# A retention and mixture-of-experts kernel: operand places within 256 bytes, and one load issued earlier

## The chip, the cores and the metric

The kernel runs on one core of a Trainium2 chip. The metric is the device time of one execution in microseconds. TensorE multiplies, VectorE (DVE) and ScalarE (ACT) do elementwise work, GpSimd (POOL) gathers and scatters rows, and SyncE (SP) issues nearly all DMAs from one queue, in order.

## The reference

Three layers in a row on 4608 tokens of width 512, all in float32:

```python
scores = scale * np.matmul(q, k.transpose(0, 1, 3, 2))       # 8 batches, 8 heads, 576 x 64
ret = scores * Dmat[None]                                    # decay gamma**(i-j), causal
x = np.matmul(ret, v)                                        # -> (4608, 512)

logits = x @ w_gate + modality_bias[modality_id]             # 8 experts, top 1
for e in range(8):
    h = np.maximum(x[mask] @ w1[e], 0.0)                     # 512 -> 1024
    out[mask] = gate_w[mask, None] * (h @ w2[e])             # 1024 -> 512

h = np.maximum(x @ w_in, 0.0)                                # 512 -> 2048
return (h * h @ w_out).astype(np.float32)                    # 2048 -> 512
```

## The kernel before

Every float32 operand of the big products is split in a high and a low part, and a product is three matmuls: high by high, high by low, low by high. In a matmul one operand is stationary (128 columns are loaded) and the other streams past it.

Stage 1 (to about 200 us) computes the retention and the routing. Stage 2 computes the experts. A unit is a slot of up to 512 tokens of one expert with one of 8 groups of 128 hidden columns; units are numbered i = 0 to 79, and the slots are 512 tokens wide, at the end 448 (i = 56 to 63), 384 (64 to 71) and 256 (72 to 79). Pass i of the loop issues `first` of unit i + 1 (lines 839 to 841; ACT makes hh at 855, VectorE hl at 856), in some passes `trans` of the next slot's tokens (ACT xh, VectorE xl, 794 and 795), then `second` of unit i, then a split of expert weights (ACT at 156, VectorE at 157) and a share of the generator `convs`. That one prepares the last stage's weights in 16 conversions (VectorE at 745 to 768, then `conv3`, which splits them in cwh and cwl and stores them). ACT, VectorE and SP each work through their queue in this order of issue. A third generator, `combos`, makes the first token sums of the last stage: its first step empties `convs`, takes two tiles and issues the load of eyr (line 802); the later steps compute on eyr. Its steps are taken at i = 65 (one) and from 66 on (two each). By the costs that `convs` gives for its pieces, four block sums and the first half of `conv3` come at i = 62 and the other half at 63.

Stage 3 (from about 616 us) is the last layer pair, in Strassen-like form: 9 blocks of 512 tokens, seven products each, hidden columns in three passes. In the first layer (`one`) the weights w are stationary and the tokens' sums x stream, 256 columns a matmul; in the second (`two`) h is stationary and the weights stream, 256 columns. Both issue their three matmuls in the helper `six` (lines 1199 to 1201). The order of all work in stage 3 is written out by a planner from fixed costs and due times; addresses play no part in it.

Where tiles stand: the pools `cv` (6 tiles of 8192 bytes in each partition), `wp` (10 of 8192), `rp` (one of 8192) and `ip` (three of 32) follow each other, and then, in stage 3, the pool with h0, h1 and h2. All tiles of `cv` and `wp`, and so x and both layers' weights, have the same place within 256 bytes; the h tiles, 14336 bytes each, stand 96 bytes beyond it. The stage-2 tiles of tokens and of h have the place of the weights.

Of the kernel before, what the change touches and what calls it, by code (L numbers as in the profile page):

```python
# [10 lines left out]
F32R = mybir.dt.float32r  # L11
# [14 lines left out]
P = 128  # L26
# [66 lines left out]
def kernel(ctx, tc, qT, kT, kN, vN, modT, w_gate, mbias, w1, w2, w_in, w_out,  # L93
# [155 lines left out]
    def route_c(g):  # L249
        t0 = G * g  # L250
        ob, ok = RS.pop(g)
        for j in range(G):
            pe.matmul(tps, ob[:, j, :], ok[:, j, :], start=(t0 + j == 0), stop=True, skip_group_check=True)

    def tab_out():
        dve.tensor_scalar(out=tab, in0=tps, scalar1=IDOFF, scalar2=None, op0=ALU.add)
# [155 lines left out]
    def run(gen, n):  # L412
        for _ in range(n):
            if next(gen, 0) == 0:
                return False
        return True

    def chain(*gens):
        for g_ in gens:
            for _ in g_:  # L420
                yield 1
# [45 lines left out]
    def gather(s):  # L467
        nt = blocks(s)
        rmax = (NTILE - G) * P if s == "E" else NT
        src = eslot[0:1, 1:2] if s == "E" else slots[0:1, 1, s:s + 1]  # L470
        reg = pool.value_load(src, min_val=0, max_val=KEYS - nt)
        ix = new(ip, [P, 4], I32, "ix", "ix")
        pool.tensor_copy(ix[:, :nt], tab[:, bass.ds(reg, nt)])
        xg = new(wp, [P, 4, DM], F32, "w", "xg")
        for j in range(nt):
            pool.indirect_dma_start(out=xg[:, j, :], out_offset=None, in_=xd[:rmax, :],
                                    in_offset=bass.IndirectOffsetOnAxis(ap=ix[:, j:j + 1], axis=0))
        XG[s] = (xg, ix)
# [236 lines left out]
    def phase12():  # L715
        ring[0] = psG
        with ExitStack() as c1:
# [79 lines left out]
            def combos():  # L797
                for _ in cs:
                    pass
                yr = cv.tile([P, KD, TS], F32, tag="w", name="eyr")  # L800
                tx = cv.tile([P, 2, 256], F32, tag="w", name="etx")
                sp.dma_start(yr, yd[:, 0:TS].rearrange("(c p) t -> p c t", p=P))
                yield 1
                xs = [cv.tile([P, 2, 2, 2, 256], F32R, tag="w", name=f"x{a}") for a in range(4)]
                b11, b12 = yr[:, 0:2, 0:256], yr[:, 0:2, 256:512]
                b21, b22 = yr[:, 2:4, 0:256], yr[:, 2:4, 256:512]

                def sub(o, a, b):
                    dve.tensor_tensor(out=o, in0=a, in1=b, op=ALU.subtract)

                def put(m, src):
                    t_ = held["x", m] = xs[m // 2][:, m % 2]
                    split(t_[:, 0], t_[:, 1], src, dve)
                    sp.dma_start(xc[0, m], t_.bitcast(F32).rearrange("p a k t -> p (a k t)"))

                sub(tx, b12, b11)
                put(0, b11)
                yield 1
                put(1, b21)
                yield 1  # L820
                sub(b12, b22, b12)
                put(2, b22)
                yield 1
                sub(b11, b22, tx)
                put(3, tx)
                yield 1
                put(5, b12)
                yield 1
                sub(b21, b21, b11)
                put(4, b11)  # L830
                yield 1
                put(6, b21)
                yield 1
# [9 lines left out]
            def first(u):  # L843
                s, f = u
                xh, xl = X[s]
                wd = width(s)
                w = W[s, f // 2][0]
                fo = slice((f % 2) * P, (f % 2) * P + P)
                ps = new(psG, [P, TS], F32, "g", "psh")[:, :wd]
                for k in range(KD):  # L850
                    three(ps, (w[:, 0, k, fo], w[:, 1, k, fo]), (xh[:, k, :wd], xl[:, k, :wd]),
                          k == 0, k == KD - 1)
                hh = new(hp, [P, TS], F32R, "hh", "hh")[:, :wd]
                hl = new(hp, [P, TS], F32R, "hl", "hl")[:, :wd]
                act.activation(hh, ps, AF.Relu)
                dve.scalar_tensor_tensor(out=hl, in0=ps, scalar=0.0, in1=hh.bitcast(F32), op0=ALU.max,  # L856
                                         op1=ALU.subtract)
                HS[u] = (hh, hl)
# [37 lines left out]
            ex = combos()  # L896
# [9 lines left out]
            def ws(upto, most=99, ldto=0):  # L906
                while most and st["sp"] < min(upto, nw):
                    wl(st["sp"] + 1)
                    wsplit(wkeys[st["sp"] // 2], st["sp"] % 2, dve)
                    st["sp"] += 1  # L910
                    most -= 1
                    wl(ldto)
# [90 lines left out]
            for i, u in enumerate(us):  # L1003
                s, f = u
                k = seq.index(s)
                nx = seq[k + 1] if k + 1 < len(seq) else None
                if nx is not None and f == (4 if s == "E" else 0):
                    gather(nx)
                if i + 1 < len(us):
                    first(us[i + 1])  # L1010
                if nx is not None:
                    if s == "E" and f == 6:
                        trans(nx, 0)
                        trans(nx, 1)
                    elif s != "E" and 3 <= f <= 6:
                        trans(nx, f - 3)
                if u == (NF, 7):
                    wload2(1, 0, wp)
                if i == 71:
                    tc.mark_branch_hint_location("extra0", 0, HINTED)  # L1020
                second(u)
                if s == "E" and f == 6:
                    trans(nx, 2)
                    trans(nx, 3)
                if i == 2:
                    route_c(last)
                if i == 0:
                    for _ in route_a(last):
                        pass
                    next(cs)  # L1030
                elif i == 1:
                    tb = table()
                    next(tb)
                    for _ in route_b(last, dve):
                        next(tb)
                elif i == 2:
                    ws(6, 2, 7)
                    tab_out()
                    turn = tab_turn()
                    next(turn)  # L1040
                    for _ in range(10):
                        next(tb)
                elif i == 3:
                    while next(tb) != "set":
                        pass
                    turn = chain(turn, tb)
                    ws(8, 2, 11)
                else:
                    wl(i + 9)
                    run(turn, 9)  # L1050
                    fill(wsg(i + 6, 2 if i < 10 else 1, i + 9), part(cs, 2250))
                    if i >= 65:
                        run(ex, 1 if i == 65 else 2)
                    if i == 73:
                        assert next(cs, 0) == 0 and next(ex, 0) == 0
                        extras()
                        wload2(0, 0, cv)
                if u == (NF, 1):
                    wload2(0, 1, wp)
                if u == (NF, 5):  # L1060
                    wload2(0, 2, wp)
                if i == 6:
                    ext = nc.values_load(slots[0:1, 3, 0:1], min_val=0, max_val=NX)
            assert st["ld"] == st["sp"] == nw

    held = {}

    def wload2(m, j, pool_, load=True):
        for x in range(2):
            held["w", m, j, x] = pool_.tile([P, 7, 256], F32R, tag="w", name=f"w{m}{j}{x}")  # L1070
            if load:
                sp.dma_start(held["w", m, j, x].bitcast(F32).rearrange("p m c -> p (m c)"), wc[m, PASSES[0][j], x])

# [73 lines left out]
    def phase3():  # L1147
        with ExitStack() as c2:
            ff = c2.enter_context(tc.tile_pool(name="ff", bufs=1))
            sb = lambda name, shape, dt=F32R: ff.tile(shape, dt, tag=name, name=name)  # L1150
# [2 lines left out]
                wload2(1, j, wp, False)  # L1153
            WT = [[[held["w", m, j, x] for x in range(2)] for j in range(3)] for m in range(2)]
            XT = [held["x", m] for m in range(7)]
            HT = [sb(f"h{j}", [P, 2, 7, 256]) for j in range(3)]
            ZT = [sb(f"z{j}", [P, 8, 256], F32) for j in range(3)]
            yr = rp.tile([P, KD, TS], F32, tag="raw", name="yr")
            xt = sb("xt", [P, 2, 256], F32)
# [91 lines left out]
            def one(n, q, x):  # L1251
# [6 lines left out]
                kx, ky, kz = ("X", u % 2), ("Y", u % 2), ("Z",)  # L1258
                z, h = ZT[u % 3], HT[u % 3]
                kz_ = lambda *i: [("z", u % 3, j) for j in i]  # L1260
# [52 lines left out]
            def two(n, x):  # L1313
# [4 lines left out]
                for q in range(len(PASSES[p])):  # L1318
                    u = HS_[n, q]
                    h, m, w, mo = HT[u % 3], MH[x], WT[1][q], MO[x]  # L1320
                    plan.add(MMS, six([ps[:, 0, :], ps[:, 1, :]],
# [108 lines left out]
```

## Time and profile before

| | |
|---|---|
| median of 3 runs | 1345.21 us (1340.93 to 1346.01) |
| profiled execution | 1348.41 us, its span 1346.5 us |
| TensorE busy | 1312.9 us, 98% of the span |
| VectorE busy | 1022.8 us, 76% |
| ScalarE busy | 624.5 us, 46% |
| TensorE's granted clock | 0.995 in the mean |

The span runs from the first to the last instruction of the profiled execution; times in rows count from its start. A matmul's start is observed and its end is modelled, so that consecutive ones overlap; the step from start to start is the price of one. DVE, ACT and POOL rows have their real duration. An SPq row is the issue of a DMA, not its transfer.

### The profile page before, as it was taken

The numbers are of one execution on the slowest core, as the hardware profiler recorded it, in microseconds if no ns is written. First come the engines' busy times: TensorE is split into PE (matmuls) and PEld (weight loads), VectorE is DVE, ScalarE is ACT, GpSimd is POOL, SyncE is SP. The second block draws the span as 40 slices with busy tenths as digits, with TensorE's granted clock in tenths as the row PEclk, the third lists the DMA queues.
The fourth block names the chain that finished last, engine by engine and source line by source line (L and its number), as shares of the span: only waits on it lengthen the run. The fifth ranks groups of instructions, "written<-read, shape, count | busy, mean of one in ns | idle before, by whom it ended". The sixth has DMA issues, their size and how long they took to land.

```text
span 1346.5 us, 26963 instructions
## 1 busy us (share of the span) xinstructions
PE 1312.9 (98%) x10639; PEld 1226.4 (91%) x10639; DVE 1022.8 (76%) x2095; ACT 624.5 (46%) x1283; POOL 125.2 (9%) x170
## 2 busy tenths in 40 slices
PE   7999989999999999999999999999999999999997
PEld 7888877888888889899999999999999999999996
DVE  3787858878787788647788888758788777776665
ACT  1444344454545545536655666534434444433343
POOL 3222112101110110000000000000000011111121
PEclk9999989999999999999999999999999999999999
DMA  9998257788787877887554445668799755655551
GB/s 330 391 351 300 77 189 237 278 279 294 246 299 244 318 263 233 295 330 294 218 208 189 173 172 204 251 257 310 282 342 342 294 203 200 211 174 173 173 188 48
DMA packets 139957, 331.90 MB, mean 246 GB/s; under 512 B 15185, under 2 KB 52849, under 8 KB 139825
## 3 DMA queue, kind: packets, MB, share of 16 engines
q1 hardware_dynamic: 132208, 309.82, 64.3%
q0 software_dynamic: 5840, 19.14, 4.0%
q8 instruction: 85, 1.39, 0.4%
q10 hardware_dynamic: 1776, 1.17, 0.3%
q14 instruction: 48, 0.39, 0.1%
HBM read 222.33 MB, written 107.78 MB: 245 GB/s over the span
## 4 chain that ended last, share of the span: by engine, by line
PE 50%; DVE 4%; ACT 1%; issue 0%; POOL 0%; POOLq 0%; DVEq 0%
PE bank L1201 17%; PE bank L1199 16%; PE bank L1200 16%; DVE z L1177 2%; DVE h L1302 1%; DVE z L1185 1%; ACT h L1301 0%; PE bank L839 0%; PE bank L841 0%; PE bank L840 0%; POOL out L1309 0%; DVE oe L1177 0%; ACT z L1174 0%; DVE x L1177 0%; DVE yr L1177 0%
## 5 line engine op out<-in xcount | busy, mean ns | idle before, releaser
L1199 PE MATMUL bank<-x,w 128*128 128x256 f32 x1008 | 286.0, 284 | 1.5 <-ACT z L1174 1.5
L1200 PE MATMUL bank<-x,w 128*128 128x256 f32 x1008 | 285.7, 283 | 0.5 <-DVE x L1177 0.5
L1199 PE MATMUL bank<-w,h 128*128 128x256 f32 x1008 | 282.8, 281 | 2.4 <-DVE oe L1177 1.6
L1201 PE MATMUL bank<-x,w 128*128 128x256 f32 x1008 | 285.0, 283 | 0.0
L1201 PE MATMUL bank<-w,h 128*128 128x256 f32 x1008 | 282.6, 280 | 1.8 <-DVE h L1302 1.8
L1200 PE MATMUL bank<-w,h 128*128 128x256 f32 x1008 | 282.4, 280 | 1.0 <-DMA w<-wc 1.0
L1174 ACT ACTIVATE z<-bank 128x256 f32<-128x256 f32 x288 | 108.8, 381 | 254.0 <-PE bank L1201 252.0
L1301 ACT ACTIVATE h<-z 128x512 fp32r<-128x512 f32 (+2 forms) x270 | 158.3, 599 | 81.8 <-DVE z L1177 65.1
L1199 PEld LDWEIGHTS bank<-x,w 128*128 128x128 f32 x1008 | 192.5, 191 | 3.1 <-ACT z L1174 3.1
L1200 PEld LDWEIGHTS bank<-x,w 128*128 128x128 f32 x1008 | 192.8, 191 | 1.1 <-DVE x L1177 0.7
L1199 PEld LDWEIGHTS bank<-w,h 128*128 128x128 f32 x1008 | 189.9, 188 | 3.7 <-DVE oe L1177 2.6
L1201 PEld LDWEIGHTS bank<-x,w 128*128 128x128 f32 x1008 | 193.1, 192 | 0.0
L1201 PEld LDWEIGHTS bank<-w,h 128*128 128x128 f32 x1008 | 189.6, 188 | 2.8 <-DVE h L1302 2.7
L1200 PEld LDWEIGHTS bank<-w,h 128*128 128x128 f32 x1008 | 189.5, 188 | 1.2 <-DMA w<-wc 1.2
L1302 DVE TENSOR_TENSOR h<-z,h 128x512 fp32r<-128x512 f32 (+2 forms) x270 | 169.0, 649 | 7.8 <-ACT h L1301 7.8
L1177 DVE TENSOR_TENSOR z<-z,bank 128x256 f32<-128x256 f32 x216 | 89.6, 417 | 69.6 <-PE bank L1201 52.6
L839 PE MATMUL bank<-hh,wy 128*128 128x512 f32 (+3 forms) x320 | 122.5, 383 | 0.0
L839 PE MATMUL bank<-xh,wx 128*128 128x512 f32 (+3 forms) x320 | 119.1, 372 | 1.7 <-DVEq L958 1.7
L840 PE MATMUL bank<-hl,wy 128*128 128x512 f32 (+3 forms) x320 | 119.3, 373 | 0.2 <-DVE hl L856 0.2
L841 PE MATMUL bank<-hh,wy 128*128 128x512 f32 (+3 forms) x320 | 119.2, 373 | 0.0
L841 PE MATMUL bank<-xh,wx 128*128 128x512 f32 (+3 forms) x320 | 118.9, 372 | 0.0
L840 PE MATMUL bank<-xl,wx 128*128 128x512 f32 (+3 forms) x320 | 118.8, 371 | 0.1
(185 smaller groups left out, 2132.5 us busy)
## 6 DMA issues: line engine op xcount, KB each, us to landing
x<-xc SPq DMA_DIRECT2D x112, 512.0 KB
wr<-w SPq DMA_DIRECT2D x80, 512.0 KB
xc<-x SPq DMA_DIRECT2D x63, 512.0 KB
w<-wc SPq DMA_DIRECT2D x32, 896.0 KB
wc<-cwh SPq DMA_DIRECT2D x16, 896.0 KB
wc<-cwl SPq DMA_DIRECT2D x16, 896.0 KB
pd<-oe SPq DMA_DIRECT2D x24, 512.0 KB
xd<-xs SPq DMA_DIRECT2D x9, 1024.0 KB
```

Of the source, the lines that this page charges most:

```text
L839: pe.matmul(ps, lh, rh, start=first, stop=False)
L840: pe.matmul(ps, lh, rl, start=False, stop=False)
L841: pe.matmul(ps, ll, rh, start=False, stop=last)
L1174: plan.add(a_(c), lambda e: e.activation(o, i, f), r, w)
L1177: plan.add(engs or d_(c), lambda e: e.tensor_tensor(out=o, in0=a, in1=b, op=op), r, w)
L1185: e.scalar_tensor_tensor(out=z, in0=z, scalar=0.0, in1=z, op0=ALU.max, op1=ALU.mult)
L1199: e.matmul(ps[n], lh, rh, start=first and n == 0, stop=False, skip_group_check=True)
L1200: e.matmul(ps[n], lh, rl, start=False, stop=False, skip_group_check=True)
L1201: e.matmul(ps[n], ll, rh, start=False, stop=True, skip_group_check=True)
L1301: plan.add(a_(c), lambda e: e.activation(h[:, 0, a:b], z[:, a + 1:b + 1], AF.Copy), rs, ks[0])
L1302: plan.add(d_(c), lambda e: e.tensor_tensor(out=h[:, 1, a:b], in0=z[:, a + 1:b + 1], in1=h[:, 0, a:b].bitcast(F32), op=ALU.subtract), rs + ...
```

## The change

The first layer's weight tiles in stage 3 (m = 0) get 32 more elements, and the weights stand 16 elements (64 bytes) into them. The second layer's weight tiles get longer too, with the weights at their start. The h tiles get 64 more elements, and h begins 56 elements (224 bytes) into them: 96 + 224 = 320, which is 64 beyond the streamed weights within 256 bytes. So in both layers what is stationary stands 64 bytes beyond what streams. The first step of `combos` is taken at i = 61 instead of 65, with nothing taken at 62 to 65.

```diff
-                    if i >= 65:
-                        run(ex, 1 if i == 65 else 2)
+                    if i == 61 or i >= 66:
+                        run(ex, 1 if i == 61 else 2)
...
         for x in range(2):
-            held["w", m, j, x] = pool_.tile([P, 7, 256], F32R, tag="w", name=f"w{m}{j}{x}")
+            o = 0 if m else 16
+            wt = pool_.tile([P, 7 * 256 + 32], F32R, tag="w", name=f"w{m}{j}{x}")
+            held["w", m, j, x] = wt[:, o:o + 7 * 256].rearrange("p (m c) -> p m c", m=7)
...
-            HT = [sb(f"h{j}", [P, 2, 7, 256]) for j in range(3)]
+            HT = [sb(f"h{j}", [P, 2 * 7 * 256 + 64])[:, 56:56 + 2 * 7 * 256]
+                  .rearrange("p (x m c) -> p x m c", x=2, m=7) for j in range(3)]
```

The token sums, whose first step is moved:

```python
            def combos():
                for _ in cs:
                    pass
                yr = cv.tile([P, KD, TS], F32, tag="w", name="eyr")
                tx = cv.tile([P, 2, 256], F32, tag="w", name="etx")
                sp.dma_start(yr, yd[:, 0:TS].rearrange("(c p) t -> p c t", p=P))
                yield 1
```

## Rows read from the trace of the kernel before

**Rows 1.** The page's first part: TensorE's busy time, share of the span, instructions.
```profile
PE 1312.9 (98%) x10639; PEld 1226.4 (91%) x10639; DVE 1022.8 (76%) x2095; ACT 624.5 (46%) x1283; POOL 125.2 (9%) x170
```

**Rows 2.** Groups by line: two of stage 3's six; busy us, mean ns, idle before.
```profile
L1199 PE MATMUL bank<-x,w 128*128 128x256 f32 x1008 | 286.0, 284 | 1.5 <-ACT z L1174 1.5
...
L1199 PE MATMUL bank<-w,h 128*128 128x256 f32 x1008 | 282.8, 281 | 2.4 <-DVE oe L1177 1.6 <-ACT h L1301 0.6
```

**Rows 3.** Timeline of TensorE, stage 3: start us, length; 24 second-layer rows, then 72 first-layer.
```profile
901.95 0.28 PE L1199 MATMUL bank<-w,h 128*128 128x256 f32 x1
...
904.65 0.28 PE L1201 MATMUL bank<-w,h 128*128 128x256 f32 x1
904.76 0.28 PE L1199 MATMUL bank<-x,w 128*128 128x256 f32 x1
...
913.28 0.28 PE L1201 MATMUL bank<-x,w 128*128 128x256 f32 x1
```

**Rows 4.** Timeline of TensorE, stage 2: 12 rows of 512 columns, 23 of 448.
```profile
301.09 0.39 PE L839 MATMUL bank<-xh,wx 128*128 128x512 f32 x1
...
303.59 0.40 PE L841 MATMUL bank<-xh,wx 128*128 128x512 f32 x1
...
517.70 0.37 PE L841 MATMUL bank<-xh,wx 128*128 128x448 f32 x1
...
522.25 0.37 PE L839 MATMUL bank<-xh,wx 128*128 128x448 f32 x1
```

**Rows 5.** Timeline of VectorE, i = 62 and 63, and its first use of eyr.
```profile
542.69 0.62 DVE L856 SCALAR_TENSOR_TENSOR hl<-bank,hh 128x448 fp32r<-128x448 f32 x1
543.23 0.55 DVE L795 TENSOR_TENSOR xl<-bank,xh 128x384 fp32r<-128x384 f32 x1
...
544.82 1.55 DVE L768 TENSOR_TENSOR cwk<-cwk 128x256 f32<-128x256 f32 x4
546.29 0.95 DVE L157 TENSOR_TENSOR cwl<-cwk,cwh 128x768 fp32r<-128x768 f32 x1
...
549.58 1.22 DVE L157 TENSOR_TENSOR cwl<-cwk,cwh 128x1024 fp32r<-128x1024 f32 x1
...
565.91 0.69 DVE L809 TENSOR_TENSOR etx<-eyr 128x512 f32<-128x512 f32 x1 [5.88 <-DMA eyr<-yd]
```

**Rows 6.** Timeline of ACT, i = 62 and 63.
```profile
539.26 0.55 ACT L855 ACTIVATE hh<-bank 128x448 fp32r<-128x448 f32 x1 [2.66 <-PE bank L841]
539.70 0.49 ACT L794 ACTIVATE xh<-bank 128x384 fp32r<-128x384 f32 x1
...
542.81 0.85 ACT L156 ACTIVATE cwh<-cwk 128x768 fp32r<-128x768 f32 x1 [1.66 <-DVE cwk L759]
...
548.31 1.05 ACT L156 ACTIVATE cwh<-cwk 128x1024 fp32r<-128x1024 f32 x1
```

**Rows 7.** Timeline of TensorE around xl of i = 62, and in two later blocks.
```profile
543.83 0.44 PE L840 MATMUL bank<-xl,wx 128*128 128x384 f32 x1
...
561.12 0.34 PE L841 MATMUL bank<-xh,wx 128*128 128x384 f32 x1
...
562.91 0.33 PE L841 MATMUL bank<-hh,wy 128*128 128x384 f32 x1
...
565.51 0.34 PE L841 MATMUL bank<-xh,wx 128*128 128x384 f32 x1
568.45 0.69 PE L792 MATMUL bank<-ident,xg 128*128 128x128 f32 x2 [2.60 <-DVE hl L856]
...
571.40 0.34 PE L841 MATMUL bank<-hh,wy 128*128 128x384 f32 x1
```

**Rows 8.** Timeline of SP's queue: the issue of the token sums' load.
```profile
556.40 0.55 SPq L802 DMA_DIRECT2D eyr<-yd  x1
```

**Rows 9.** Windows: us; busy PE, PEld, DVE, ACT, POOL; granted clock, DMA share, GB/s.
```profile
566.00:592.00 26.00, 21.89 (x139) 21.62 (x139) 19.49 (x29) 16.36 (x29) 0.00 (x0) 0.93 0.79 275
...
1053.00:1346.50 293.50, 281.88 (x2347) 278.97 (x2346) 205.74 (x438) 117.46 (x275) 39.01 (x71) 0.99 0.53 185
```

## The prediction, made before the result

> **What bounds the kernel now.** I read the page first. TensorE is busy for 98% of the span [rows 1], so what can move the end is either a shorter step from one matmul to the next or a shorter idle of TensorE. Next come the groups by line: the third stage holds 6 groups of 1008 matmuls, 3 of the first layer (weights stationary, tokens streaming) and 3 of the second (h stationary, weights streaming), equal in shape [rows 2]. The mean of one there is a modelled length that overlaps its neighbours, so I took the step from starts in the timeline. A run of the first layer takes 8.52 us for 71 steps, 120.0 ns each; a run of the second 2.70 us for 23 steps, 117.4 ns each [rows 3]. Same shape, same clock, and the two differ by 2.6 ns. What the program has different is the place: x and first-layer weights stand on the same offset within 256 bytes, h stands 96 bytes beyond the weights that stream past it.
>
> In the stage before, everything stands at offset 0. There 512 columns step by 227.3 ns (11 steps in 2.50 us) [rows 4]. 256 more columns thus cost 107 ns, so 256 columns alone are about 107 ns, and 13 ns of the 120 go to something else; in the second layer 10. These 10 to 13 ns are all that a placement can touch. The price is not fixed by the offset alone: 448 columns at offset 0 should take 120.0 + 192/256 x 107.3 = 200.5 ns and take 206.8 (22 steps in 4.55 us) [rows 4].
>
> Last I read the timelines of the three engines around the token sums, 541 to 572 us [rows 5 to 8]. The load is issued at 556.40, and VectorE waits 5.88 us for it, to 565.91. Its queue is in order, so hl stands behind, and TensorE is idle for 2.60 us before 568.45 [rows 5, 7, 8]. [...] From the first-layer matmul at 565.51 to the ninth second-layer one after it are 5.89 us; the same stretch one block before took 1.79 (561.12 to 562.91). The late load costs 4.1 us [rows 7].
>
> **First-layer weights, offset 0 to 64.** No instruction is added, the tiles only get longer. The trace has no row at 64. From below, the step can't fall under the 107 ns of streaming; from above, the dearest row at this kind of work is the 448-column run, 6.3 ns over, so 126.3 [rows 3, 4]. The nearest row is the second layer at offset 96: 117.4. I take it, because 64 too parts two streams that now start level. 3 x 1008 = 3024 matmuls [rows 2] x 2.6 ns = **-7.9 us**. TensorE is nearly the only bound there: from 1053 us to the end it is busy for 281.9 of 293.5 us, and part of the rest is the closing stores [rows 9], so nearly all of this reaches the end.
>
> **h, offset 96 to 64.** Between the same ends, 107 and 126.3. Nearest row: itself at 96. I take 117.4 again, **0 us**. If 64 lies on the straight line between 0 and 96, each layer costs 118.3: -5.1 and +2.7.
>
> Other engines write h and the loaded weights 64 bytes elsewhere. I put that at 0: those ACT and VectorE operations take whole rows as before, and the DMAs carry the same rows. A loss there would be covered by the idle quarter of VectorE [rows 1]; without that cover 1% of its 1022.8 us would be 10 us. A gain I exclude, as they are not the bound.
>
> [...]
>
> **Token sums' load, from i = 65 to i = 61.** The generator's first step does more than load. It first empties the conversion generator, of which at i = 61 six pieces are left: four 256-column sums (1.55 us) and the two splits with their ACT copies, which now come at i = 62 and 63 [rows 5, 6]. Then it queues the two stores of that conversion and the load. All are issued four blocks earlier, or five before the first use. Three queues are crossed.
>
> *SP*: the load now stands behind the two stores, which wait for the last split (about 546.4), and the weight loads of i = 62 on stand behind it. It should be issued near 547.6 rather than 556.4; with the 9.5 us that it took it lands by 557 or so, ahead of its use. The 5.88 us of VectorE and **4.1 us** on TensorE go. A weight load is late by about 4 us (1 MB at the 275 GB/s of [rows 9]); weights are split several blocks ahead, which covers it. POOL is not crossed.
>
> *ACT and VectorE*: here something new is late. VectorE is full at that place: from 538 to 548 its operations touch. In ACT's queue hh of the next block (539.26), then xh of column group 3 (539.70), now stand behind both cwh copies [rows 6]. The first starts as now at 542.81, when its source is done, the second for the four sums, which now run from 542.7 to 544.2. So: cwh 542.8 to 543.65, cwh 544.2 to 545.25, hh to 545.75, xh to 546.2. On VectorE: the sums to 544.2, cwl (0.95) to 545.1, cwl (1.22) from 545.25 to 546.45, hl (0.62) to 547.0, xl (0.55) to 547.55 [rows 5, 6]. TensorE's next first-layer group needs that xl: its matmul that started at 543.83, right when xl came, starts at 547.55, **3.7 us later** [rows 7]. The idle is as long as the one now at 568, so the clock may fall too: there, of the 4.1 us, 2.6 were idle and 1.5 the slow steps after [rows 7]. I add 0.6, less than half, since one matmul comes in between when xh is there. The bounds of this stall are 0 (if the queues are not as I read them) and 3.7 + 1.5 = 5.2 us. From 548 to 566 VectorE has room, so the delay is carried on, not made worse. Sum of this part: -4.1 + 4.3 = **+0.2 us**. The stall moves, it doesn't go.
>
> **Sum.** -7.9 + 0 + 0.2 = -7.7 us. The profiled execution took 1348.41 us, 1346.5 in the span and 1.9 around it; it would become 1340.7. It lies 3.2 us over the median of the runs, 1345.21; on the median the sum gives **1337.5 us**.
>
> **Rivals.**
>
> *64 is cheaper than either.* Both layers halfway between 107 and 120, 113.4 ns: 3024 x 6.6 + 3024 x 4.0 = 32.1 us, with +0.2: 1313 us. For it: within the second layer and at changes between layers single steps of 0.11 us occur (904.65 to 904.76) [rows 3], so the 10 ns are not a fixed toll. Against it: no run of steps so short.
>
> *The offset does nothing.* The 2.6 ns then belong to something else that differs between the layers (the bank they write, who wrote the operand last). For it: 448 columns cost 6.3 ns more without a change of offset [rows 4]. Against it: the first layer holds 120.0 over 71 steps in a row, just as the stage before at the same offset 0. 1345.2 + 0.2 = 1345.4 us. [...]
>
> *The slower side: 64 falls in with 0.* The mechanism is the second layer losing its good place: its step goes to 120.0 while the first layer stays at 120.0, +7.9 us, 1353.3 us (+0.6%). It decides from the point where the second layer's step rises by more than the first's falls. For it: 96 is the only place at which steps under 118 were seen in a run. At the far end, both at 126.3, it would be 19 + 27 us, 1391; I keep that end out, since no 256-column run shows it.
>
> *The early pieces are hidden*, or the early stall has a longer wake: 1333.2 to about 1338; this is inside my own case.
>
> **How the numbers follow.** My case has 0.42 (1331 to 1342, by 0.7 ns a step for one layer and by the load's bounds), cheaper 0.28, nothing 0.18, slower 0.12. The range 1310 to 1350 holds my case, the unmoved one, some 0.17 of the cheaper and a little of the slower, 0.8 together. A measurement here tells about 0.5% from no change, 6.7 us, so faster means under 1338.5: 0.28 and a bit over half of my case, 0.54. Slower (over 1351.9): most of that rival, 0.09. The rest, 0.37.
>
> **What would show it.** Runs of first-layer steps at 117 ns instead of 120; second-layer steps unmoved; the load issued near 547 and no VectorE wait for it; hl and xl near 546.5 instead of 542.7, and a TensorE idle near 544 to 547 in place of the one at 565 to 568. I am wrong if first-layer runs stay at 120, if either layer falls below 115 or rises over 119, or if the block after i = 61 shows no stall.

## The result, and the profile after

The changed kernel took 1330.49 us in the median of eight runs (1325.12 to 1336.09), against 1343.62 us for the kernel before in the same group of runs: a ratio of 0.9906, interval 0.9876 to 0.9935, or 13 us less. The forecast was 1337.5 us in a range of 1310 to 1350. Direction and range hold; the gain is 13 instead of 8 us, and three of the terms behind it were wrong in size.

The profiled execution of the changed kernel took 1335.92 us, its span 1334.1 us, 12.4 less than before's 1346.5. The first part of its page answers to [rows 1]; TensorE loses 17 us of busy time, VectorE 2:

```profile
PE 1295.9 (97%) x10639; PEld 1209.8 (91%) x10639; DVE 1020.9 (77%) x2095; ACT 624.1 (47%) x1283; POOL 125.2 (9%) x170
```

I split the 12.4 us by the start of the same matmul in both traces: both hold the 10639 in the same order. A positive lag means that the changed kernel is later.

| matmul | before, us | after, us | lag, us |
|---|---|---|---|
| a `second` matmul of 512 columns, ahead of the moved load | 504.25 | 505.52 | +1.27 |
| the last ones ahead of the new stall (number 4180 of 10639) | 540.41 | 541.64 | +1.23 |
| just after it (4200) | 544.49 | 550.19 | +5.71 |
| twenty later (4220; the same lag up to 4320) | 548.30 | 556.25 | +7.95 |
| past the old stall (4340; the same up to 4440) | 572.96 | 576.85 | +3.89 |
| first of stage 3 | 607.91 | 611.51 | +3.60 |
| last of stage 3 | 1338.94 | 1326.47 | -12.47 |

The first 1.27 us are there from the start of the kernel (a load of stage 1) and belong to no edit. The load's move then **costs** 2.3 us (3.60 - 1.27), and stage 3 **gives** 16.1 us: 731.03 us from its first matmul to its last before, 714.96 after. A single trace is not sharp to a microsecond: in the kernel with the load alone (below), whose stage 3 is that of before with the same steps, that stretch took 727.10 us.

**Stage 3.** Here is the timeline of TensorE in the changed kernel, start and length in us, as are those below; the matmul lines 1199 to 1201 of before are 1202 to 1204 here, and each "..." hides matmuls of the same kind.

```profile
611.51 0.28 PE L1202 MATMUL bank<-x,w 128*128 128x256 f32 x1
...
941.55 0.28 PE L1202 MATMUL bank<-x,w 128*128 128x256 f32 x1
...
943.59 0.28 PE L1202 MATMUL bank<-x,w 128*128 128x256 f32 x1
...
950.62 0.36 PE L1204 MATMUL bank<-w,h 128*128 128x256 f32 x1
950.82 0.28 PE L1202 MATMUL bank<-w,h 128*128 128x256 f32 x1
951.19 0.39 PE L1202 MATMUL bank<-w,h 128*128 128x256 f32 x1
951.42 0.28 PE L1203 MATMUL bank<-w,h 128*128 128x256 f32 x1
...
958.36 0.28 PE L1202 MATMUL bank<-w,h 128*128 128x256 f32 x1
...
961.07 0.28 PE L1204 MATMUL bank<-w,h 128*128 128x256 f32 x1
...
1326.47 0.28 PE L1204 MATMUL bank<-w,h 128*128 128x256 f32 x1
```

From 941.55 to 943.59 are 18 steps: 113.3 ns each, where [rows 3] has 120.0. From 958.36 to 961.07 are 23 steps: 117.8 ns, where [rows 3] has 117.4. The two prices don't belong to the two layers. Up to about 631 us both layers go at 117.8, from 633 to 951 both at 113.3, after that both at 117.8 again, but for a few us near 1053 and the last ones from about 1320 on. The switch near 951 us stands right behind the uneven steps of 950.62 to 951.42 (0.20, 0.37 and 0.23 us); the profile names no wait there. The mean over the stage (steps under 135 ns between matmuls of one layer) is 115.8 ns in the first layer and 115.7 in the second, where before has 119.8 and 117.4. 3024 x 4.0 + 3024 x 1.7 = 17.2 us; the other 1.1 us of the difference to 16.1 lie outside these steps.

**The load.** SP's timeline in the changed kernel shows it issued at 548.36 instead of 556.40 [rows 8], right behind a store of the conversion, and that of VectorE shows its first use:

```profile
547.99 0.32 SPq L778 DMA_DIRECT2D wc<-cwl  x1
548.36 0.90 SPq L802 DMA_DIRECT2D eyr<-yd  x1
```

```profile
547.88 0.61 DVE L856 SCALAR_TENSOR_TENSOR hl<-bank,hh 128x448 fp32r<-128x448 f32 x1
548.41 0.55 DVE L795 TENSOR_TENSOR xl<-bank,xh 128x384 fp32r<-128x384 f32 x1
...
567.91 0.69 DVE L809 TENSOR_TENSOR etx<-eyr 128x512 f32<-128x512 f32 x1
```

The 5.88 us that VectorE waited [rows 5] are gone: the last row has no bracket. But hl and xl start 5.2 us later than in [rows 5], behind the conversion pieces that were pulled ahead. TensorE's timeline shows what that does; the bracket is the idle time before, and what ended it:

```profile
544.47 0.34 PE L841 MATMUL bank<-xh,wx 128*128 128x384 f32 x1
547.57 0.44 PE L839 MATMUL bank<-xh,wx 128*128 128x384 f32 x1 [2.76 <-ACT xh L794]
549.01 0.69 PE L840 MATMUL bank<-xl,wx 128*128 128x384 f32 x1 [1.00 <-DVE xl L795]
...
549.82 0.58 PE L839 MATMUL bank<-hh,wy 128*128 128x448 f32 x1
...
553.93 0.57 PE L841 MATMUL bank<-hh,wy 128*128 128x448 f32 x1
```

It waits 2.76 us for xh and then 1.00 for xl. After that 448 columns step by 373.6 ns (11 steps from 549.82 to 553.93), where [rows 4] has 206.8. The windows give the clock (us, busy PE, PEld, DVE, ACT, POOL, granted clock, DMA share, GB/s):

```profile
548.00:557.00 9.00, 8.00 (x29) 7.47 (x29) 3.58 (x5) 4.11 (x8) 0.00 (x0) 0.62 1.01 350
...
566.00:592.00 26.00, 26.00 (x167) 25.86 (x166) 19.04 (x29) 15.84 (x28) 0.00 (x0) 1.00 0.83 288
```

From 548 to 557 us the granted clock is 0.62; within that, from 548.40 to 555.10, it is 0.50. From 566 to 592, where [rows 9] has 0.93 and the old stall, it is 1.00. In the kernel before, the low stretch stood behind the old stall:

```profile
568.50:571.40 2.90, 2.90 (x11) 2.90 (x12) 2.88 (x5) 2.90 (x7) 0.00 (x0) 0.53 0.88 331
571.40:576.00 4.60, 4.60 (x29) 4.56 (x29) 4.60 (x8) 2.61 (x5) 0.00 (x0) 1.00 0.92 341
```

### The profile page after: what moved, and what is told of

Same layout as the page of the kernel before. It is cut to its first block, busy times and chain, and to the rows that moved or that the text cites. A ratio compares the mean times of both kernels' runs of the same rounds, so it can differ in the third digit from the quotient of the medians.

```text
span 1334.1 us, 26958 instructions
## 1 busy us (share of the span) xinstructions
PE 1295.9 (97%) x10639; PEld 1209.8 (91%) x10639; DVE 1020.9 (77%) x2095; ACT 624.1 (47%) x1283; POOL 125.2 (9%) x170
## 4 chain that ended last, share of the span: by engine, by line
PE 43%; DVE 10%; DMA 1%; issue 1%; POOL 0%; POOLq 0%; ACT 0%; DVEq 0%
PE bank L1203 14%; PE bank L1202 14%; PE bank L1204 14%; DVE z L1180 4%; DVE h L1305 3%; DVE z L1188 1%; DVE x L1180 1%; DVE yr L1180 1%; DMA w<-wc 1%; PE bank L839 0%; PE bank L840 0%; PE bank L841 0%; POOL out L1312 0%; DVE oe L1180 0%; POOLq L1429 0%
## 5 line engine op out<-in xcount | busy, mean ns | idle before, releaser
L1203 PE MATMUL bank<-x,w 128*128 128x256 f32 x1008 | 282.0, 280 | 3.2 <-DVE x L1180 3.2
L1204 PE MATMUL bank<-x,w 128*128 128x256 f32 x1008 | 281.4, 279 | 0.1
L1202 PE MATMUL bank<-x,w 128*128 128x256 f32 x1008 | 281.3, 279 | 0.0
L1203 PEld LDWEIGHTS bank<-x,w 128*128 128x128 f32 x1008 | 189.3, 188 | 4.5 <-DVE x L1180 4.5
L1204 PEld LDWEIGHTS bank<-x,w 128*128 128x128 f32 x1008 | 191.6, 190 | 0.3 <-DMA w<-wc 0.3
L1202 PEld LDWEIGHTS bank<-x,w 128*128 128x128 f32 x1008 | 189.5, 188 | 0.0
L840 PE MATMUL bank<-hl,wy 128*128 128x512 f32 (+3 forms) x320 | 119.9, 375 | 0.2 <-DVE hl L856 0.2
```

What stands on the lines that cost most here:

```text
L840: pe.matmul(ps, lh, rl, start=False, stop=False)
L1202: e.matmul(ps[n], lh, rh, start=first and n == 0, stop=False, skip_group_check=True)
L1203: e.matmul(ps[n], lh, rl, start=False, stop=False, skip_group_check=True)
L1204: e.matmul(ps[n], ll, rh, start=False, stop=True, skip_group_check=True)
```

## Experiments

Three questions: which edit carries the gain, why 64, and can the load move without a stall. Each group below shared its runs of the kernel before. Means of a step are those of the profiled execution, first and second layer, taken as above (before: 119.8 and 117.4 ns). In the experiments that move the weights the tiles get 64 more elements where the change has 32; their slots hold 8192 bytes in either case, so the places are the same.

**One part alone: the load.** The places are those of before, the load is issued at i = 61.

```diff
-                    if i >= 65:
-                        run(ex, 1 if i == 65 else 2)
+                    if i == 61 or i >= 66:
+                        run(ex, 1 if i == 61 else 2)
```

> Only the load of the token sums is moved to i = 61; all places as before. My theory (the stall moves to the block after i = 61 and, with the lower clock after it, costs a little more than it saves): +1 to +4 us against the kernel before, VectorE's wait for eyr gone, a TensorE idle of 3 to 4 us near 545. Rival (the early pieces are hidden and the 4.1 us are saved): -3 to -5 us, no such idle. The steps of both layers stay at 120 and 117.4 ns.

Measured: 1346.41 against 1344.22 us, ratio 1.0014 (1.0005 to 1.0023); steps 119.8 and 117.4. TensorE's timeline in this kernel has the same stall, with the same releasers:

```profile
545.56 0.44 PE L839 MATMUL bank<-xh,wx 128*128 128x384 f32 x1 [2.75 <-ACT xh L794]
547.01 0.69 PE L840 MATMUL bank<-xl,wx 128*128 128x384 f32 x1 [1.01 <-DVE xl L795]
```

By lag, as in the table above, the new stall costs 5.24 us here (-0.77 to +4.47), and the old one, gone, gives 4.10 (+4.50 to +0.40). So the move to 61 is a small loss, as in the changed kernel.

**One part alone: both places.** Weights and h at 64, the load at i = 65.

```diff
-                    if i == 61 or i >= 66:
-                        run(ex, 1 if i == 61 else 2)
+                    if i >= 65:
+                        run(ex, 1 if i == 65 else 2)
```
(against the changed kernel)

> Only the places are changed (first-layer weights and h both 64 bytes beyond what streams); the load stays at i = 65. If the places carry all of the gain: -12 to -22 us, and steps at 113 or near 118 ns in both layers, changing between the two only after an idle of TensorE. If the load carried a part of it: clearly less than the 13 us of the whole change.

Measured: 1323.25 us (1320.46 to 1336.89), ratio 0.9873 (0.9841 to 0.9904); 114.4 and 114.4 ns. Stage 3 goes from 604.60 to 1310.90, 706.3 us, 24.7 less than before. The places alone carry the whole gain: 17 us by the ratio, 21 by the medians.

**One place alone: the weights.** h stays 96 beyond.

```diff
-            HT = [sb(f"h{j}", [P, 2 * 7 * 256 + 64])[:, 56:56 + 2 * 7 * 256]
-                  .rearrange("p (x m c) -> p x m c", x=2, m=7) for j in range(3)]
+            HT = [sb(f"h{j}", [P, 2, 7, 256]) for j in range(3)]
```
(against the changed kernel, the load at 65 again)

> Only the first-layer weights are moved, to 64 beyond the tokens; h stays at 96. If each layer's step follows its own offset: first layer 113 to 118 instead of 120, second unchanged at 117.4, -6 to -20 us. If the short step of 113 needs both layers at the same offset (a timing that one layer hands to the other): first layer 118, second 117 to 118, about -6 us.

Measured: 1335.09 us, ratio 0.9929 (0.9916 to 0.9941); 113.9 and 119.9 ns. The first layer falls by 5.9 ns, and the second, of which nothing was moved, rises by 2.5. Neither reading of the forecast had that rise. TensorE's timeline shows a run of each layer:

```profile
905.10 0.28 PE L1203 MATMUL bank<-x,w 128*128 128x256 f32 x1
...
907.82 0.28 PE L1203 MATMUL bank<-x,w 128*128 128x256 f32 x1
...
919.30 0.28 PE L1201 MATMUL bank<-w,h 128*128 128x256 f32 x1
...
922.06 0.28 PE L1203 MATMUL bank<-w,h 128*128 128x256 f32 x1
```

In the first layer 24 steps in 2.72 us are 113.3 ns; only up to 618 us does it go at 117.8. In the second 23 steps in 2.76 us are 120.0 ns, where [rows 3] has 117.4 for the same operands at the same places. By steps, -5.9 x 3024 + 2.5 x 3024 = -10.3 us; by time, -9.1.

**One place alone: h.** The weights stay at 0.

```diff
-            o = 0 if m else 16
-            wt = pool_.tile([P, 7 * 256 + 32], F32R, tag="w", name=f"w{m}{j}{x}")
-            held["w", m, j, x] = wt[:, o:o + 7 * 256].rearrange("p (m c) -> p m c", m=7)
+            held["w", m, j, x] = pool_.tile([P, 7, 256], F32R, tag="w", name=f"w{m}{j}{x}")
```
(against the changed kernel, the load at 65 again)

> Only h is moved, from 96 to 64 beyond the streaming weights; first-layer weights stay level with the tokens. If each layer's step follows its own offset: first layer 120, second 113 to 118, 0 to -12 us. If the short step needs both: second layer about 118, 0 to +2 us.

Measured: 1344.72 us, ratio 1.0002 (0.9993 to 1.0011); 120.0 and 117.65. The second layer now has exactly the places that it has in the changed kernel. It goes at 117.8 ns, the dearer of its two prices there, almost throughout; the cheaper one comes in three short stretches near 629, 632 and 1329 us. TensorE's timeline has the second of them, and the first-layer matmul that ends it:

```profile
631.58 0.28 PE L1202 MATMUL bank<-w,h 128*128 128x256 f32 x1
...
632.94 0.28 PE L1202 MATMUL bank<-w,h 128*128 128x256 f32 x1
633.05 0.28 PE L1200 MATMUL bank<-x,w 128*128 128x256 f32 x1
...
633.89 0.28 PE L1201 MATMUL bank<-x,w 128*128 128x256 f32 x1
```

12 steps in 1.36 us are 113.3 ns; the first layer then steps by 120.0 (7 steps in 0.84 us), and the second comes back at 117.8. The number fits both readings of the forecast (113 to 118, and about 118). What the two runs show together: a layer at 64 has the same two prices whether or not the other layer is moved, but with the first layer at 0 the second doesn't keep the cheaper one, and the second at 96 gets dearer when the first is moved. So what a layer costs is not set by its own places alone: weights alone give 9 us, h alone nothing, both together 17.

**The load two passes later.** Places as in the changed kernel, the load at i = 63, where `convs` has nothing left that must be pulled ahead.

```diff
-                    if i == 61 or i >= 66:
-                        run(ex, 1 if i == 61 else 2)
+                    if i == 63 or i >= 66:
+                        run(ex, 1 if i == 63 else 2)
```

> Both places as in the change, the load at i = 63, where the conversion generator ends by itself, so nothing is drawn forward. My theory (the late load costs about 4 us of TensorE, the early emptying of the generator costs as much): both stalls gone, no idle over 1 us on TensorE between 535 and 575, 3 to 5 us off the places alone before the spread of the two step prices (113 and 118 ns), so about 1316 to 1332. Rival (the load is late again, or its two stores and itself hold up the weight loads): an idle of over 2 us at the first use or at a weight split, no gain over the places alone.

Measured: 1333.37 against 1350.32 us, ratio 0.9875 (0.986 to 0.989); 115.15 and 114.95 ns. The stalls are gone as forecast. The 3 to 5 us off the places alone are not shown: the ratio is that of the places alone (0.9873).

The same kernel and the changed one once more, sharing their runs of before:

> The change with the load at i = 63. Without the early stall and the late load, and with the same draw of step prices: 4 to 7 us under the change itself on the same chip (ratio to before lower by 0.003 to 0.005). Rival (the load's place is worth nothing once the places are right): no difference that stands out of the spread.

> The change as it is, once more, beside the same with the load at i = 63, on one chip. The step price of stage 3 is drawn anew after each idle of TensorE between 113.3 and 117.8 ns: single runs between 1318 and 1338 on a chip where the kernel before takes 1344, mean ratio 0.987 to 0.993. The early stall near 545 is there in every run.

Measured, against 1347.48 us: 1332.39 with the load at 63, ratio 0.9892 (0.9873 to 0.991), and 1340.67 with it at 61, ratio 0.9941 (0.9921 to 0.9962). The intervals don't overlap; between the ratios lie 0.0049, 6.6 us (8.3 between the medians), as forecast. Part of that can be chance, since in the profiled executions the steps were 115.1 against 116.4 ns too. The repeat of the changed kernel missed its forecast: the ratio lies over 0.993, and its runs (1334.63 to 1341.98) reach past 1338, though before is 3.5 us slower here than the 1344 that the forecast assumed, which explains the runs and not the ratio. The trace of the load at 63 is the clearer witness. Its waits of TensorE from 535 to 590 us (total, times, longest), and its window:

```profile
PE bank L839 <- DVEq L958: 1.4, 1, 1.4
```

```profile
535.00:590.00 55.00, 53.49 (x325) 51.77 (x324) 39.59 (x55) 29.96 (x50) 0.00 (x0) 1.00 0.84 300
```

Waits and window of the changed kernel in the same stretch:

```profile
PE bank L839 <- ACT xh L794: 2.8, 1, 2.8
PE bank L840 <- DVE xl L795: 1.0, 1, 1.0
```

```profile
535.00:590.00 55.00, 51.24 (x282) 49.35 (x282) 37.27 (x52) 28.30 (x48) 0.00 (x0) 0.94 0.81 279
```

With the load at 63 neither the early stall nor the late one is there. What is left is a wait of 1.4 us for VectorE's queue (L958), which the kernel before has too (1.7 us), and the clock is 1.00 instead of 0.94. VectorE's timeline and SP's show that the load is still late:

```profile
551.65 1.12 SPq L802 DMA_DIRECT2D eyr<-yd  x1
```

```profile
562.48 0.69 DVE L809 TENSOR_TENSOR etx<-eyr 128x512 f32<-128x512 f32 x1 [2.36 <-DMA eyr<-yd]
```

VectorE waits 2.36 us for it, and nothing that TensorE needs is late for that. The lag to before goes from +0.10 us ahead of this stretch to -3.80 behind it: the 3.9 us that a load in time is worth against this one execution of before.

**Other distances.** The same distance O in both layers, the load at 65. The weight tiles' slots stay as they are.

```diff
-            o = 0 if m else 16
-            wt = pool_.tile([P, 7 * 256 + 32], F32R, tag="w", name=f"w{m}{j}{x}")
+            o = 0 if m else O // 4
+            wt = pool_.tile([P, 7 * 256 + 64], F32R, tag="w", name=f"w{m}{j}{x}")
...
-            HT = [sb(f"h{j}", [P, 2 * 7 * 256 + 64])[:, 56:56 + 2 * 7 * 256]
+            e = (O - 96) % 256 // 4
+            HT = [sb(f"h{j}", [P, 2 * 7 * 256 + 64])[:, e:e + 2 * 7 * 256]
```
(against the changed kernel, the load at 65 again)

> Both places at 32 bytes instead of 64, the load at 65 as before. If any distance between the streams will do: steps of 113 to 118 ns in both layers. If 64 is special: steps between 117 and 120.

> Both places at 128 bytes, the load at 65 as before. If the streams repeat their relation every 128 bytes: as level ones, 120 ns. If every 256: some other price, 113 to 118.

> Both places at 192 bytes, the load at 65. If the relation repeats every 128 bytes: steps of 113.3 or 117.8 ns as at 64, -10 to -20 us. If it repeats every 256: a price of its own, no 113.3.

> Both places at 80 bytes, the load at 65. If the short step belongs to a stretch of distances around 64: 113.3 alone or with 117.8. If to 64 alone: 117 to 120 throughout, within 5 us of before.

| distance | us | ratio to before | mean step | prices seen |
|---|---|---|---|---|
| 32 | 1348.85 | 0.9993 (0.9984 to 1.0003) | 118.4, 118.3 | one |
| 64 (load at 65, load at 63) | 1323.25, 1333.37 | 0.9873, 0.9875 | 114.4 to 115.15 | 113.3 and 117.8 |
| 80 | 1348.99 | 1.0016 (1.0004 to 1.0027) | 119.0, 119.0 | 118.7 and 119.8 |
| 128 | 1351.42 | 1.0005 (0.9995 to 1.0014) | 119.1, 119.1 | 118.6 and 120.0 |
| 192 | 1343.59 | 0.9971 (0.996 to 0.9983) | 117.3, 117.4 | 113.3 and 117.8, mostly 117.8 |

Of these only 64 and 192 have the short price, and 192 holds it seldom: the prices came as in its first reading, the 10 to 20 us didn't. The 119.1 ns at 128 fit neither of the readings given for it. A distance "somewhere between" is worth nothing: 32, 80 and 128 are within 0.2% of before. The same 0 or the same 96 in both layers, 160 and 320 were not tried.

**The same distance in stage 2.** As with the load at 63, and the streamed token and h tiles xh, xl, hh and hl begin 192 bytes (48 elements) further in, so that the experts' weights stand 64 beyond them.

```diff
-                hh = new(hp, [P, TS], F32R, "hh", "hh")[:, :wd]
-                hl = new(hp, [P, TS], F32R, "hl", "hl")[:, :wd]
+                hh, hl = (shift(hp, n, 1)[:, :wd] for n in ("hh", "hl"))
...
+            def shift(pool_, n, k):
...
+                t_ = pool_.tile([P, k * TS + 64], F32R, tag=n, name=n)[:, 48:48 + k * TS]
```
(xh and xl in the same way, with k = KD)

> As the run with the load at 63, and in the expert stage too what streams (tokens and h, high and low) is moved so that the expert weights stand 64 bytes beyond it. If the price of a place is a property of the two streams and not of the last stage: the step at 512 columns falls from 227 to 220 to 225 ns, 3 to 13 us off. If it belongs to 256-column steps alone: 227 stays, 0 us.

Measured: 1339.09 us, ratio 0.9921 (0.9908 to 0.9935), against 0.9875 without it: it costs about 6 us. TensorE's timeline of this kernel in stage 2:

```profile
300.55 0.40 PE L847 MATMUL bank<-hh,wy 128*128 128x512 f32 x1
...
303.82 0.40 PE L846 MATMUL bank<-xl,wx 128*128 128x512 f32 x1
```

14 steps in 3.27 us are 233.6 ns, where [rows 4] has 227.3. Neither reading had a loss. But the last slots of stage 2 are 256 columns wide, and there the step falls. TensorE's timeline of this kernel in those slots:

```profile
598.31 0.28 PE L845 MATMUL bank<-hh,wy 128*128 128x256 f32 x1
...
602.28 0.28 PE L847 MATMUL bank<-hh,wy 128*128 128x256 f32 x1
```

And in the kernel before:

```profile
597.83 0.28 PE L839 MATMUL bank<-xh,wx 128*128 128x256 f32 x1
...
602.03 0.28 PE L841 MATMUL bank<-xh,wx 128*128 128x256 f32 x1
```

35 steps each, in 3.97 and 4.20 us: 113.4 ns against 120.0. In the mean over the stage, 256 columns go from 119.8 to 113.6 ns, 384 and 448 change by about 1 ns, and 512 go from 227.5 to 233.3. So the short price belongs to matmuls of 256 columns and not to stage 3; and since here the streamed operands were moved and the stationary ones not, it goes with the distance of the two. What is good for 256 columns is bad for 512.

## Why the prediction was right in direction and short in size

**What bounds the kernel: right.** The gain came out where the step from matmul to matmul became shorter, and nearly all of it reached the end: 17.2 us of steps, 16.1 us of stage 3. One row was read high: the 206.8 ns of 448 columns, from which the upper end of 126.3 was made, lie at the top of the stage (203.6 ns in the mean, 202 to 207 over a dozen steps).

**First-layer weights, -7.9 us: right sign, mis-sized.** The term took the nearest row, the second layer at 117.4 ns, as the price at 64. It measured 115.8 in the mean, and more to the point no single price: 113.3 or 117.8, changing within a run. "I am wrong if either layer falls below 115" came true. By the first layer alone the term is -12.1 us, by both -17.2.

**h, 0 us: the step that failed.** I priced each layer from its own places. Weights without h show that this is not how it works: the second layer went from 117.4 to 119.9 with nothing of its own moved. Moving h on top of that brought it to the price of the first. In the changed kernel the second layer is thus 4.2 ns x 3024 = 12.7 us cheaper than with the weights alone, but the first is dearer (115.8 against 113.9 ns, 5.7 us), so h is worth about 7 us there. By times it is 8 (17 for both places less 9 for the weights alone), and alone it is worth nothing (ratio 1.0002).

**The rivals.** "64 is cheaper than either" put 113.4 ns on both layers, and the lower of the two prices is 113.3. It was half true: the changed kernel has that price for less than half of the stage (115.75 lies 0.46 of the way from 117.8 to 113.3). "The offset does nothing" falls with 32, 80 and 128, where the same tiles with another distance give nothing, and with the weights alone. "64 falls in with 0" happened in no run at 64 and 64, but its mechanism, the second layer rising to 120, did with the weights alone.

No run shows a stretch of steps under 113.3 ns; the 107 ns that the forecast has as the lower end is its author's estimate from [rows 3, 4]. With the distance the mean over the stage goes from 119.1 ns (128) to 114.4 (64, the load at 65).

**The load: mechanism right, clock part mis-sized.** The stall came where the text had it, for the operands it named. This execution was 1.2 us late already; less that, xh's matmul starts at 546.3 and xl's at 547.8, where 546.2 and 547.55 were written, and the load is issued at 547.1, where 547.6 was written. The gain at the old place is right for the execution that it was read from: 4.1 us were written, and the lag falls by 4.08 (+7.97 at matmul 4320 to +3.89 at 4340). (That price is partly chance, as the end of this part shows.) The price of the new stall is not: 4.3 us were written, 3.7 idle and 0.6 for the clock, and the lag rises by 6.72, 4.48 of it up to matmul 4200 and 2.24 in the twenty after it, which up to 555.1 us run at the granted clock of 0.50. In the repeat of the changed kernel the same stall cost 6.33 us (-0.49 to +5.84), in the kernel with the load alone 5.24, which was the upper bound of the forecast. The two idle times are 3.76 us together in the changed kernel and in the one with the load alone; what is over them, 3.0 and 1.5 us, is the part of the slow steps, not 0.6. "The stall moves, it doesn't go" is shown, and what it costs extra is the slow clock after it. From the first lag of stage 2 to stage 3 the term is +2.3 us, not +0.2 (some 0.3 come back near 590 us, in the kernel with the load alone too).

What the late load costs varies from execution to execution. Matmuls 4320 to 4340 take 3.35 to 3.37 us where the load was moved. In the eight traces with the load at 65 they take 7.15 to 7.56 us six times, but 5.66 (both places) and 5.95 us (distance 128) in the other two: 2.3 to 4.2 us in all. The stall is there each time, the lower clock isn't. TensorE's timeline and a window at distance 32:

```profile
568.08 0.69 PE L792 MATMUL bank<-ident,xg 128*128 128x128 f32 x2 [2.09 <-DVE hl L856]
```

```profile
564.00:574.00 10.00, 7.91 (x38) 7.58 (x37) 8.40 (x14) 6.48 (x12) 0.00 (x0) 0.83 0.72 257
```

And at 128:

```profile
567.62 0.44 PE L792 MATMUL bank<-ident,xg 128*128 128x128 f32 x2 [2.38 <-DVE hl L856]
```

```profile
564.00:574.00 10.00, 7.62 (x46) 7.14 (x45) 8.86 (x14) 8.15 (x15) 0.00 (x0) 1.00 0.70 251
```

After 2.09 us of idle the granted clock is 0.83 in its window, after 2.38 us it stays at 1.00. So the length of the idle alone doesn't say whether the clock falls.

**The sum.** Predicted -7.9 + 0 + 0.2 = -7.7. Measured in the spans: +1.3 (stage 1, no edit) + 2.3 - 16.1 = -12.5. That the first group gained 13 us is in part a draw of the two prices: the repeat of the changed kernel gained 7 to 8. The range and the direction hold for both.

**Why the times are so wide apart.** The changed kernel ran from 1325 to 1336 us in one group of runs and from 1335 to 1342 in another, where the kernel before is 3.9 us slower. In six profiled executions at 64 and 64 I looked for each change of price (a mean over 12 steps, so to within about 1.4 us). There were 52, and each was seen within 1.8 us after a step of more than 126 ns. These traces hold 414 such longer steps, so most change nothing; that the price is drawn anew after each idle, as the forecast of the repeat has it, is not shown. How much of the stage goes at 113.3 then differs from run to run: 114.4 ns in the mean with both places alone (profiled time 1320.5 us), 116.4 in the repeat of the changed kernel (1341.83). 2.0 ns x 6048 steps are 12 of those 21 us. Of the rest 4.6 are in stage 3 too (706.3 against 722.99 us), in longer steps, and 4.8 ahead of it, where stage 3 starts at 604.60 and 609.39. That the unprofiled runs spread for this reason is argued; they have no trace. What chooses the price after a longer step stays open, and so does why a distance has its price.

**The better version.** Both places with the load at i = 63: ratios of 0.9875 and 0.9892, ahead of before and, where they ran side by side, of the changed kernel (0.9941). Whether it also beats both places with the load at 65 (0.9873, in another group) these runs can't tell.

## What to carry to other kernels

Where TensorE is the bound, measure the step between starts for each kind of matmul and try the distance of its two operands (32, 64, 80, 128 and 192 bytes were run here; that the relation repeats every 256 is not shown), for all kinds that follow each other at once: an edit of one kind can move the price of another (here from 117.4 to 119.9 ns). Take nothing over from one width to the next (at 64, 256 columns gained 6.2 ns and 512 lost 5.8), and look at several runs, since one place can have two prices (113.3 and 117.8 ns). When a load is issued earlier through a generator, count what that generator must finish first; here a load two passes earlier than before was early enough for TensorE and pulled nothing ahead.

## What the runs showed of the hardware that was not expected

- At a distance of 64 bytes a matmul of 256 columns has two prices, 113.3 and 117.8 ns. With both layers at 64 they have the same one at any time; each holds for up to 318 us and changes only right behind a step of over 126 ns (52 of 52 changes, 414 such steps).
- What one layer's matmuls cost depends on the places of the other's: with h and the streamed weights unmoved, the second layer rose from 117.4 to 119.9 ns when the first layer's weights moved from 0 to 64. With h alone at 64 the second layer had the cheaper price for three short stretches only.
- The order of distances is not smooth: 118.4 ns at 32, about 115 at 64, 119.0 at 80, 119.1 at 128, 117.3 at 192.
- At 64 in stage 2, 512 columns step by 233.3 ns instead of 227.5, and 256 columns by 113.6 instead of 119.8.
- Two waits of 2.76 and 1.00 us with one matmul between them were followed by a granted clock of 0.50 from 548.40 to 555.10 us, in which 448 columns stepped by 373.6 ns instead of 206.8. The same stall cost 5.2, 6.3 and 6.7 us in three executions; from 546 to 555 us the granted clock was 0.81 in the first and 0.63 in the other two.
- With one idle of 2.0 to 2.6 us, the same in eight traces, matmuls 4320 to 4340 took 7.15 to 7.56 us in six and 5.66 and 5.95 in two (idle 2.1 and 2.4 us). From 564 to 574 us the granted clock was 0.83 at distance 32 (idle 2.09 us) and 1.00 at 128 (2.38 us).
